# FFN output weights loaded ahead of batch three's values, and a Hankel tile of which half is loaded and half copied

## The chip, the cores and the metric

The kernel runs on one core of a Trainium2 chip. The core has five engines with their own instruction streams: TensorE (PE, matmuls, with weight loads shown as PEld), VectorE (DVE), ScalarE (ACT), GpSimd (POOL) and SyncE (SP). They wait for each other by semaphores. SP, ACT and POOL also issue DMAs. The metric is the device time of one execution in microseconds (us).

## What is computed

Attention with a relative position bias for 8 batches of 8 heads, 576 positions and 64 numbers a head, and behind it a feed-forward network (FFN) in which three products are joined by a maximum:

```
scores = q @ k.T / sqrt(64) + bias[bucket(|i - j|)]      # per batch and head, 576 x 576
x      = softmax(scores) @ v                             # to (8*576, 512)
h      = max(x @ w1, x @ w2, x @ w3)                     # w: 512 x 768
out    = h @ w_out                                       # w_out: 768 x 512, out: 4608 x 512, float32
```

The bucket depends on the distance |i - j| alone, and is the same for all distances from 128 up.

## The kernel before

**Bias as a product.** Softmax doesn't change when a constant is taken from all scores, so the kernel uses exp(bias - bias at far distance) as a factor: it is 1 from distance 128 up, and differs only in a band of 383 diagonals. `spread_bias` makes for each of the 8 heads a row of 511 such factors, w_sb, and writes it to DRAM (w_dr). `load_hank` reads it back as a Hankel tile, `hank`: partition p holds the row shifted by p. The exponentials of the scores are multiplied by slices of it on DVE (`times_band`, L771; `times_band_left`, L870; and `times_bandt`, L857, with `bandt`, a reversed copy of a part of hank that `make_bandt` writes).

**Tiling.** Keys and queries of a batch are 4 tiles of 128 positions and a tail of 64. Heads are worked in pairs (HP = 4 pairs a batch). For a pair: scores into PSUM (`sc`; `sct` for the 64 left keys, `scq` for the 64 left queries), exponentials on ACT into `e` and `el`, band products on DVE, then `attend` (products with the values, PSUM tile `a`) and the division on DVE into x_sb.

**Batches.** In batch 0 the queries and keys are turned on PE (`first_transposes`, `more_transposes`), in two passes over the four pairs: the first takes queries 0 to 255, the second the others. Batch 1 is turned on PE too. From batch 2 on, SP turns queries and keys by DMA transposes (L702, ten a batch, for tiles 0 to 3 and the tail, queries and keys by turns); from batch 1 on it also turns the attention's output x_sb into xT (L923, L971). xT, 128 x 4 x 4608, is the FFN's input; corners of it that are written late hold other data early on (borrowed for q and k in float32, for the indices and the zeros).

**FFN.** Its products (`ps`, `psp`, and `pso` with the output weights wo_bf) are put between the attention's as filling for PE. The first chunk of outputs comes in batch 2.

**Order.** The kernel writes the order of nearly all instructions by hand (`inorder`, `in_turn`): each engine follows program order. POOL issues the loads from DRAM that convert float32 to bfloat16: L181 and L162, L184 (queries and keys of a batch and their tails, eleven DMAs by `load_qk`), L153 and L172 (values and their tails, six by `load_v`), L1014 (FFN weights) and L1033 (output weights). A POOL load first waits for the load eight before it, whose semaphore it takes over. `go_behind` adds a wait on a given transpose to loads. In batch 1, pair 2, the order on POOL is: values of batch 2, output weights, queries and keys of batch 3, the first behind batch 2's key transpose of tile 1, the others behind that of tile 3:

```
last_v = load_v(b + 1, 0, H, turned_qk[b + 1, 1, min(b, 2) if b < 4 else KT - 1])
if b == 1:
    load_last_weights(turned_qk[2, 1, KT - 1])
    batch[3] = load_tiles()
    load_qk(3, turned_qk[2, 1, KT - 1])
```

In the first pass of batch 0, on DVE, the band products of pairs 0 and 1 (`bands`) follow the query copy of `more_transposes(0)`; the query copy of the second pass, bandt and the divisions come after them.

Of the kernel before, what the change touches and what calls it, by code (L numbers as in the profile page):

```python
# [11 lines left out]
BF16 = mybir.dt.bfloat16  # L12
# [27 lines left out]
def kernel(  # L40
# [12 lines left out]
    nc = tc.nc  # L53
    B, H, S, D = q.shape
    d_model, d_ff = moe_w1.shape
    NB = bias_table.shape[0]
    P = 128
# [5 lines left out]
    KT = 4  # L63
# [4 lines left out]
    CH = 512  # L68
    NCH = NTOK // CH
    BAND = 3 * P  # L70
    HALF = 2 * P - 1
    WL = 2 * HALF + 1
# [3 lines left out]
    const = ctx.enter_context(tc.tile_pool(name="const", bufs=1))  # L76
    stage = ctx.enter_context(tc.tile_pool(name="stage", bufs=1))
# [28 lines left out]
    def mm(*args, **kw):  # L106
        made = inorder(nc.tensor.matmul(*args, **kw))  # L107
        return made
# [11 lines left out]
    def act_copy(out_, in_):  # L120
        return inorder(nc.scalar.activation(out=out_, in_=in_, func=ACTF.Copy))

    def dve_copy(out_, in_):
        return inorder(nc.vector.tensor_copy(out_, in_))  # L124
# [22 lines left out]
    def in_turn(b, load):  # L147
        return inorder(load)

    def load_main(src, b, h0, h1, dst, t0=0, t1=KT):  # L150
        x = main_part(src, b)
        return [
            in_turn(b, nc.gpsimd.dma_start(out=dst[:, t, h0:h1, :], in_=x[:, t, h0:h1, :])) for t in range(t0, t1)  # L153
        ]
# [15 lines left out]
    def load_tail(src, b, h0, h1, dst):  # L170
        return [
            in_turn(b, nc.gpsimd.dma_start(out=dst(b, par, h0, h1), in_=tail_part(src, b, h0, h1, par)))  # L172
            for par in range(2)
        ]
# [13 lines left out]
    def go_behind(loads, behind):  # L188

        for load in loads if behind else ():  # L190
            tc.add_manual_dep(
                load.ins, behind.ins.name,
                mybir.DependencyInfo(mybir.DependencyClass.Sync, mybir.DependencyReason.DATA),
                reason="these loads go behind the transposes in line",
            )

    def load_v(b, h0, h1, behind=None):
        loads = load_main(v, b, h0, h1, vx[b % 2][:, :, :, 0:D]) + load_tail(v, b, h0, h1, v_diag)
        go_behind(loads, behind)
        return loads[-1]  # L200
# [3 lines left out]
    xT = const.tile([P, DCH, NTOK], BF16, name="xT")  # L204
# [63 lines left out]
    for vv in range(single, NB):  # L268
# [5 lines left out]
        out=pick[:, 0:NW], in0=pick[:, 0:NW], scalar1=pick[:, NW:], scalar2=None, op0=ALU.is_equal,  # L274
# [18 lines left out]
        mm(warm[:, 0:CH], lhsT=zeros[:, 0:P], rhs=zeros[:])  # L293

    act_copy(batch[0][0][:, 0:2, 0:2, :], q32[:, :, 0:2, :])
    w_sb = stage.tile([H, WL], BF16, name="w_sb")

    def spread_bias():
        spread = ps_a.tile([H, NW], F32, tag="a", name="spread")
# [7 lines left out]
        inorder(nc.scalar.dma_start(out=w_dr[:], in_=w_sb[:]))  # L307

    w_dr = dram.tile([H, WL], BF16, name="w_dr")
    hank = const.tile([P, H, BAND], BF16, name="hank")  # L310

    def load_hank(h0, h1):
        inorder(nc.sync.dma_start(
            out=hank[:, h0:h1, :],
            in_=bass.AP(
                tensor=w_dr.tensor, offset=w_dr.offset + h0 * WL,
                ap=[[1, P], [WL, h1 - h0], [1, BAND]],
            ),
        ))

# [444 lines left out]
    def times_band(hp, e4, t, lo, hi, put=lambda x: x):  # L767
        lo, hi = max(lo, P * t - P), min(hi, P * t + 2 * P)
        if lo < hi:
            c0, c1 = BAND - (hi - P * t + P), BAND - (lo - P * t + P)  # L770
            put(nc.vector.tensor_tensor(  # L771
                out=e4[:, t, :, lo:hi], in0=e4[:, t, :, lo:hi],
                in1=hank[:, 2 * hp : 2 * hp + 2, c0:c1][:, :, ::-1], op=ALU.mult,
            ))
# [36 lines left out]
    def visit(qT, kT, e4, c, mid=None, el=None):  # L811

        if el is not None:
            banks = [ps_a.tile([P, KT * 64], F32, tag="a", name="scq") for _ in range(2)]
            turn_left_queries(qT, kT, banks)
            put_left_queries(el, banks)
        for tt in range(0, KT, 2):
            scores(qT, kT, e4, c, tt)
            if tt == 0 and mid:
                mid()  # L820
# [53 lines left out]
    divided, turned_qk = {}, {}  # L874

    def attend(b, hp, e4, el, half):

        x = ps_a.tile([P, 6, AW], F32, tag="a", name="a")
        v, vl = vx[b % 2], vt[b % 2]
        for i in range(2):
            t = 2 * half + i
            c = slice(P * t, P * t + P)
            mm(
                x[:, 2 * i : 2 * i + 2, :], lhsT=el[:, c], rhs=vl[:, hp, :, 0:AW],
                start=True, stop=False, skip_group_check=True,
            )
            for par in range(2):  # L890
                for kt in range(KT):
                    mm(
                        x[:, 2 * i + par, :], lhsT=e4[:, kt, par, c], rhs=v[:, kt, 2 * hp + par, 0:AW],
                        start=False, stop=(kt == KT - 1), skip_group_check=True,
                    )
        n = 2 + half
        if half:
            mm(
                x[:, 4:6, :], lhsT=el[:, S - P : S], rhs=vl[:, hp, :, 0:AW],
                start=True, stop=False, skip_group_check=True,  # L900
            )
            for par in range(2):
                for kt in range(KT):
                    mm(
                        x[:, 4 + par, :], lhsT=el[:, S - 64 + P * kt + 64 * par :][:, 0:P],
                        rhs=v[:, kt, 2 * hp + par, 0:AW],
                        start=False, stop=(kt == KT - 1), skip_group_check=True,
                    )

        def quotients():  # L910
            rd = nrm.tile([P, 6], F32, tag="rd", name="rd")
            inorder(nc.vector.reciprocal(rd[:, 0 : 2 * n], x[:, 0 : 2 * n, D]))
            divided[b, hp, half] = inorder(nc.vector.tensor_tensor(
                out=x_sb[b][:, 2 * half : 2 * half + n, P * hp : P * hp + P].rearrange("p t (h d) -> p t h d", d=D),
                in0=x[:, 0 : 2 * n, 0:D].rearrange("p (t h) d -> p t h d", h=2),
                in1=rd[:, 0 : 2 * n].rearrange("p (t h) -> p t h", h=2).unsqueeze(3).to_broadcast([P, n, 2, D]),
                op=ALU.mult,
            ))
            if b and hp == HP - 1:
                for t in range(2 * half, 2 * half + 2 + half):  # L920
                    c = b * S + P * t
                    w = min(P, S - P * t)
                    inorder(nc.sync.dma_start_transpose(out=xT[:, :, c : c + w], in_=x_sb[b][P - w :, t, :]))  # L923
        return quotients
# [69 lines left out]
    def e_tiles():  # L994
        return (
            ep.tile([P, KT, 2, QM], BF16, tag="e4", name="e4"),
            ep.tile([P, S + KT * P], BF16, tag="el", name="el"),
        )
# [19 lines left out]
    wo_bf = const.tile([P, FCH, d_model], BF16, name="wo_bf")  # L1018
# [10 lines left out]
        load_v(1, 0, H)  # L1029
        load_w(2)  # L1030

    def load_last_weights(behind):
        load = in_turn(0, nc.gpsimd.dma_start(out=wo_bf[:], in_=moe_w_out.rearrange("(c p) m -> p c m", p=P)))  # L1033
        go_behind([load], behind)

    def bands(hp):
        for t in range(KT):
            times_band(hp, first_e[hp], t, 0, QS, inorder)
# [9 lines left out]
    for hp in range(HP):  # L1048
        qT, kT = (x[:, hp, :] for x in qk[0])
        e4, el = e_tiles()  # L1050
        first_e.append(e4)
        visit(qT, kT, e4, 0, (lambda: first_transposes(hp + 1)) if 0 < hp < HP - 1 else None)
        if hp == HP - 1:
            more_transposes(0)
        if hp == 0:
            first_transposes(1)
        if hp == 1:
            last_keys()
        if hp + 2 < HP:
            cast_keys(hp + 2)  # L1060
        if hp == HP - 1:
            bands(0)
            bands(1)
        late.append(lambda hp=hp, e4=e4, el=el: attend(0, hp, e4, el, 0))
        keep_warm()
        lefts.append(lambda hp=hp, qT=qT, kT=kT, el=el: left_keys(
            hp, qT, kT, el, 0, QS, ps_a.tile([P, QS], F32, tag="a", name="sct")
        ))
        while hp and lefts:
            lefts.pop(0)()  # L1070
# [8 lines left out]
    behind, begun = [], []  # L1079
# [69 lines left out]
    for b, hp in [(b, hp) for b in range(1, B) for hp in range(HP)]:  # L1149
# [132 lines left out]
        if hp == 1 and b > 1:  # L1282
            pending.extend((n, [fn]) for n, fn in rest)
            rest.clear()
            made, tail = ffn((b - 1) * CH, CH, False, [(b + (i + 2) // HP, (i + 2) % HP) >= ROWS for i in range(HP)])
        if hp == 2 and b + 1 < B:
            last_v = load_v(b + 1, 0, H, turned_qk[b + 1, 1, min(b, 2) if b < 4 else KT - 1])
            if b == 1:
                load_last_weights(turned_qk[2, 1, KT - 1])
                batch[3] = load_tiles()  # L1290
                load_qk(3, turned_qk[2, 1, KT - 1])
        if hp == 2 and 1 < b < B - 2:
# [73 lines left out]
```

## Time and profile before

| what | value |
|---|---|
| median of 3 runs | 312.76 us (312.24 to 314.45) |
| profiled execution | 312.26 us, of which the span of instructions is 310.5 us |
| PE busy | 298.9 us (96% of the span) |
| weight loads (PEld) | 182.5 us (59%) |
| DVE busy | 207.7 us (67%) |
| ACT busy | 202.4 us (65%) |
| POOL busy | 110.9 us (36%) |
| DMA | 40.48 MB in 163950 packets |
| chain that ended last | PE 89%, ACT 5%, DMA 2% |

A share of busy time is a mean over the whole span. Lines of a timeline give start, length, engine, line, operation, tile written <- tiles read, shape and count, and in brackets the idle time of the engine before it and what ended that. In a list of DMAs the last number is the time from issue to landing. All times are us from the start of the span.

### The profile page before, as it was taken

How to read it: one execution, taken by the hardware profiler on the slowest of the kernel's cores; microseconds unless marked ns; L12 is line 12 of the kernel's file. 1: busy time of each engine (PE TensorE's matmuls, PEld its weight loads, DVE VectorE, ACT ScalarE, POOL GpSimd, SP SyncE). 2: the span in 40 equal slices, each digit the busy share in tenths (PEclk: the TensorE clock that was granted, in tenths of full speed). 3: DMA queues.
4: the chain of work that ended last, by engine and by line, in shares of the span. 5: the costliest groups of instructions: out<-in, count | busy, mean ns of one | idle time of the engine just before them, and what ended most of it. 6: DMA issues, size and time to landing. Idle time of an engine off the chain costs nothing.

```text
span 310.5 us, 10532 instructions
## 1 busy us (share of the span) xinstructions
PE 298.9 (96%) x4542; PEld 182.5 (59%) x4542; DVE 207.7 (67%) x475; ACT 202.4 (65%) x268; POOL 110.9 (36%) x147
## 2 busy tenths in 40 slices
PE   6989999999999999999999999989999999999995
PEld 2357777775555655657665756666667654444442
DVE  7389788776777776776777667766776665553552
ACT  3899988886778777767776877675776730122211
POOL 8978752951096008900647024901500000000000
PEclk9599999999999999999999999999999999999999
DMA  9999999999999999999999999999932014202003
GB/s 167 198 187 199 182 163 136 145 166 139 141 157 191 151 187 155 133 147 198 105 101 125 165 183 111 112 146 202 131 62 106 36 33 80 101 0 103 34 0 135
DMA packets 163950, 40.48 MB, mean 130 GB/s; under 512 B 153784, under 2 KB 159424, under 8 KB 163904
## 3 DMA queue, kind: packets, MB, share of 16 engines
q0 software_dynamic: 103840, 16.66, 75.7%
q1 hardware_dynamic: 58304, 22.69, 43.6%
q8 instruction: 35, 0.57, 0.8%
q10 hardware_dynamic: 1760, 0.47, 0.7%
q14 instruction: 11, 0.09, 0.1%
HBM read 35.39 MB, written 9.45 MB: 144 GB/s over the span
## 4 chain that ended last, share of the span: by engine, by line
PE 89%; ACT 5%; DMA 2%; issue 1%; DVE 1%; ACTq 1%; DVEq 0%
PE psp L107 34%; PE ps L107 19%; PE a L107 14%; PE sc L107 9%; PE pso L107 6%; ACT e L777 4%; PE sct L107 2%; PE scq L107 2%; PE tp L111 1%; DMA xT<-in_q_dram 1%; DMA out_dram<-osb 1%; ACT el L777 1%; ACTq L213 1%; PE xp L111 0%; DVE k_sb L124 0%
## 5 line engine op out<-in xcount | busy, mean ns | idle before, releaser
L777 ACT ACTIVATE e<-sc 128x1024 bf16<-128x1024 f32 x128 | 128.4, 1023 | 30.4 <-PE sc L107 27.3
L107 PEld LDWEIGHTS <-w_bf 64*128 64x128 bf16 (+1 forms) x1088 | 73.4, 95 | 57.9 <-issue 5.0
L107 PE MATMUL psp<-xT,w_bf 64*128 64x512 bf16 x736 | 91.9, 376 | 1.9 <-issue 1.8
L771 DVE TENSOR_TENSOR e<-e,hank 128x512 bf16<-128x512 bf16 (+2 forms) x136 | 62.3, 473 | 20.3 <-ACT e L777 19.7
L107 PE MATMUL ps<-xT,w_bf 128*128 128x512 bf16 (+1 forms) x352 | 65.6, 336 | 0.0
L153 POOL DMA_DIRECT2D vx<-in_v_dram x28 | 24.7, 895 | 83.0 <-DMA kT<-k_sb 40.7
L107 PE MATMUL sc<-qT,kT 64*128 64x256 bf16 (+1 forms) x384 | 48.6, 312 | 2.0 <-DVE kT L124 0.8
L107 PEld LDWEIGHTS <-kT 64*128 64x128 bf16 (+1 forms) x736 | 31.3, 95 | 26.8 <-issue 8.4
L107 PE MATMUL a<-vx,e 64*128 64x65 bf16 (+1 forms) x1536 | 44.7, 191 | 0.0
L107 PEld LDWEIGHTS <-e 64*128 64x128 bf16 (+1 forms) x1536 | 40.7, 95 | 3.7 <-issue 0.2
L107 PEld LDWEIGHTS <-hT 64*128 64x128 bf16 (+1 forms) x444 | 26.9, 95 | 19.4 <-DVE hT L519 1.9
L107 PE MATMUL a<-vt,el 64*128 64x65 bf16 (+1 forms) x240 | 30.8, 201 | 0.4 <-DVE m L484 0.4
L107 PEld LDWEIGHTS <-el 64*128 64x128 bf16 (+1 forms) x624 | 26.2, 95 | 7.9 <-issue 4.7
L394 ACT ACTIVATE m<-ps 128x512 bf16<-128x512 f32 x14 | 8.4, 597 | 34.3 <-PE ps L107 34.3
L777 ACT ACTIVATE el<-sct 128x576 bf16<-128x576 f32 (+2 forms) x36 | 21.6, 603 | 13.5 <-PE sct L107 13.1
L107 PE MATMUL psp<-wo_bf,hT 64*128 64x256 bf16 (+1 forms) x336 | 29.7, 307 | 0.0
L181 POOL DMA_DIRECT2D q_sb<-in_q_dram x24 | 22.1, 921 | 10.7 <-issue 4.6
L181 POOL DMA_DIRECT2D k_sb<-in_k_dram x24 | 22.0, 917 | 4.0 <-DMA wo_bf<-in_moe_w_out_dram 2.1
L107 PE MATMUL pso<-wo_bf,hT 128*128 128x512 bf16 (+2 forms) x108 | 23.2, 367 | 0.0
L777 ACT ACTIVATE el<-scq 128x512 bf16<-128x512 f32 (+1 forms) x33 | 19.2, 585 | 3.3 <-PE scq L107 3.2
L403 DVE TENSOR_TENSOR m<-ps,m 128x512 bf16<-128x512 f32 x14 | 9.7, 692 | 17.0 <-PE ps L107 17.0
L519 DVE TENSOR_TENSOR hT<-psp,m 128x1024 bf16<-128x1024 f32 x12 | 14.7, 1225 | 6.9 <-PE psp L107 6.9
(82 smaller groups left out, 287.6 us busy)
## 6 DMA issues: line engine op xcount, KB each, us to landing
out_dram<-osb SPq DMA_DIRECT2D x35, 256.0 KB, 2.8
vx<-in_v_dram POOLq DMA_DIRECT2D x28, 128.0 KB, 5.0
q_sb<-in_q_dram POOLq DMA_DIRECT2D x26, 128.0 KB, 7.6
k_sb<-in_k_dram POOLq DMA_DIRECT2D x24, 128.0 KB, 7.8
w_bf<-in_moe_w_dram POOLq DMA_DIRECT2D x3, 768.0 KB, 9.3
xT<-in_k_dram SPq DMA_DIRECT2D x6, 128.0 KB, 4.2
hank<-w_dr SPq DMA_DIRECT2D x2, 384.0 KB, 5.7
wo_bf<-in_moe_w_out_dram POOLq DMA_DIRECT2D x1, 768.0 KB, 8.8
```

The costliest lines, as they stand in the source:

```text
L107: made = inorder(nc.tensor.matmul(*args, **kw))
L111: inorder(nc.tensor.transpose(*args))
L153: in_turn(b, nc.gpsimd.dma_start(out=dst[:, t, h0:h1, :], in_=x[:, t, h0:h1, :])) for t in range(t0, t1)
L181: loads.append(in_turn(b, nc.gpsimd.dma_start(out=dst[:, t], in_=main_part(src, b)[:, t])))
L213: inorder(eng.dma_start(out=dst[:, :, h, :], in_=main_part(src, 0)[:, 0:nt, h, :]))
L394: nc.scalar.activation(out=st[fb]["m0"][:], in_=ps0, func=ACTF.Copy)
L403: inorder(nc.vector.tensor_tensor(out=m[:], in0=ps1, in1=st[fb]["m0"][:], op=ALU.max))
L519: return lambda: inorder(nc.vector.tensor_tensor(out=hT[:, fb * CH : fb * CH + 2 * CH].rearrange("p (i t) -> p i t", i=2), in0=ps2(), in1= ...
L771: put(nc.vector.tensor_tensor(out=e4[:, t, :, lo:hi], in0=e4[:, t, :, lo:hi], in1=hank[:, 2 * hp : 2 * hp + 2, c0:c1][:, :, ::-1], op=ALU. ...
L777: made = nc.scalar.activation(out=out_, in_=in_, func=ACTF.Exp, scale=inv_sqrt_d)
```

## The change

The Hankel tile gets 64 more columns. The load fills partitions 0 to 63 only, with the wider rows; DVE copies each half of the heads to partitions 64 to 127, shifted by 64 columns. The first copy stands ahead of the first band products, the second behind those of pair 1. The row of factors, w_sb, moves from a tile of its own into a corner of xT, which makes room for the columns. The load of the output weights stands ahead of the values of batch 2 (`b + 1` with b = 1) in POOL's order, so right behind batch 2's queries and keys, and no longer waits for a transpose.

```diff
-    w_sb = stage.tile([H, WL], BF16, name="w_sb")
+    w_sb = xT[0:H, 0, 3 * CH + P : 3 * CH + P + WL]
...
-    hank = const.tile([P, H, BAND], BF16, name="hank")
+    hank = const.tile([P, H, BAND + 64], BF16, name="hank")
 
     def load_hank(h0, h1):
         inorder(nc.sync.dma_start(
-            out=hank[:, h0:h1, :],
+            out=hank[0:64, h0:h1, :],
             in_=bass.AP(
                 tensor=w_dr.tensor, offset=w_dr.offset + h0 * WL,
-                ap=[[1, P], [WL, h1 - h0], [1, BAND]],
+                ap=[[1, 64], [WL, h1 - h0], [1, BAND + 64]],
             ),
         ))
+
+    def copy_hank(h0, h1):
+        dve_copy(hank[64:, h0:h1, 0:BAND], hank[0:64, h0:h1, 64:])
...
-    def load_last_weights(behind):
-        load = in_turn(0, nc.gpsimd.dma_start(out=wo_bf[:], in_=moe_w_out.rearrange("(c p) m -> p c m", p=P)))
-        go_behind([load], behind)
+    def load_last_weights():
+        in_turn(0, nc.gpsimd.dma_start(out=wo_bf[:], in_=moe_w_out.rearrange("(c p) m -> p c m", p=P)))
...
         if hp == HP - 1:
+            copy_hank(0, KT)
             bands(0)
             bands(1)
+            copy_hank(KT, H)
...
         if hp == 2 and b + 1 < B:
+            if b == 1:
+                load_last_weights()
             last_v = load_v(b + 1, 0, H, turned_qk[b + 1, 1, min(b, 2) if b < 4 else KT - 1])
             if b == 1:
-                load_last_weights(turned_qk[2, 1, KT - 1])
                 batch[3] = load_tiles()
                 load_qk(3, turned_qk[2, 1, KT - 1])
```

## The prediction

> **What bounds the kernel now.** I read the page first (shares, slices), then the table by stage, then the timelines of VectorE (DVE), GpSimd (POOL) and SyncE (SP) where the two edits lie, and the times of DMAs to landing.
>
> The page says who is full, and when:
>
> ```profile
> span 310.5 us, 10532 instructions
> PE 298.9 (96%) x4542; PEld 182.5 (59%) x4542; DVE 207.7 (67%) x475; ACT 202.4 (65%) x268; POOL 110.9 (36%) x147
> PE   6989999999999999999999999989999999999995
> DVE  7389788776777776776777667766776665553552
> ```
>
> TensorE (PE) is busy 298.9 of 310.5 us. All that any edit could win from its waits is 11.6 us, and most of that lies at the two ends. So the question is where an edit makes PE wait, or stops it waiting. By stage:
>
> ```profile
> 16.00:20.00 4.00, 2.69 (x44) 1.73 (x43) 3.23 (x12) 3.95 (x7) 2.78 (x5) 1.00 1.79 181
> 20.00:24.00 4.00, 3.84 (x82) 2.89 (x81) 3.93 (x15) 3.87 (x7) 2.35 (x4) 1.00 1.44 192
> 24.00:28.00 4.00, 3.68 (x74) 2.64 (x73) 3.93 (x14) 3.80 (x7) 3.41 (x5) 1.00 1.26 209
> 56.00:64.00 8.00, 8.00 (x117) 6.02 (x115) 5.58 (x16) 7.15 (x11) 7.50 (x10) 1.00 1.70 148
> ```
>
> The columns are window, length, then busy us of PE, weight loads, DVE, ACT, POOL. From 16 to 20 us ACT is full (3.95 of 4.00) and PE waits for it: its 1.31 us idle are exponentials. From 20 to 28 DVE and ACT are both full. At 56 to 64 PE has no gap at all.
>
> The Hankel copies land here:
>
> ```profile
> 16.12 0.33 DVE L124 COPY qT<-tp 128x320 bf16<-128x320 bf16 x1 [1.63 <-PE tp L111]
> 16.36 1.83 DVE L771 TENSOR_TENSOR e<-e,hank 128x512 bf16<-128x512 bf16 x6
> 18.10 0.32 DVE L124 COPY qT<-tp 128x320 bf16<-128x320 bf16 x1
> 18.34 0.71 DVE L124 COPY bandt<-hank 64x768 bf16<-64x768 bf16 x2
> 19.65 0.18 DVE L912 RECIPROCAL rd<-a 128x4 f32<-128x4 f32 x1 [0.60 <-PE a L107]
> ```
>
> DVE has one gap, 0.60 us, before 19.65; the next is 0.43 us at 30.8. And the output weights lie here:
>
> ```profile
> 44.37 1.25 POOL L184 DMA_DIRECT2D ktail<-in_k_dram  x2
> 57.96 0.85 POOL L1033 DMA_DIRECT2D wo_bf<-in_moe_w_out_dram  x1 [0.50 <-DMA kT<-k_sb]
> 67.02 0.88 POOL L181 DMA_DIRECT2D k_sb<-in_k_dram  x1 [2.09 <-DMA wo_bf<-in_moe_w_out_dram]
> 55.40 1.21 SPq L702 DMA_TRANSPOSE kT<-ktail  x1
> kT<-ktail SPq DMA_TRANSPOSE x1, 6.0
> 62.31 0.41 PE L107 MATMUL sct<-qT,kT 128*128 128x512 bf16 x2
> 68.62 1.46 PE L107 MATMUL pso<-wo_bf,hT 128*128 128x512 bf16 x6
> ```
>
> The output weights are issued at 57.96 and land after 8.8 us, at 66.8; their first reader starts at 68.62, so PE does not wait for them. The last key transpose of batch two is issued at 55.40, lands after 6.0, at 61.4, and its reader's weight load starts at 62.20: 0.8 us of cover, the thinnest near this edit.
>
> [...] 512 elements take 0.28 us (the packed copies at L228), 768 take 0.35 (bandt). [...] I don't take the halved Hankel load as landing much sooner. [...] the trace has one band product of 839 ns beside POOL's copies at 25.4 us, where the median is 426. [...] the third query transpose of batch two, with POOL's queue nearly empty, lands in 4.0 us, the first of batch three, beside loads, in 8.9 to 10.2.
>
> **Part one, the Hankel tile.** *Removed:* per load, 512 rows of 768 bytes become 256 rows of 896 bytes; over both, 786 KB become 459 KB. Before, the two land at 15.2 (10.0 + 5.2) and 16.6 (10.4 + 6.2), their readers come at 16.36 and 18.34, so nothing waits for them. Loads behind on the same engines may come some tenths sooner; PE is held by ACT there, so I count zero, and at most 0.3 us.
>
> *Added:* two DVE copies of 64 x 1536 elements. Price: [...] from the trace's slope, 0.35 + 768 x (0.07/256) = 0.56. Back to back copies overlap by some 0.06, so 0.50 each. From below they cannot be free; from above, [...] 1.0 each, twice the price.
>
> *Where it lands:* the first sits between the query copy and the first bands. Bands of pair 0 end at 17.3 + 0.5 = 17.8, their reader `a` starts at 18.85: covered. The second sits ahead of the query copy at 18.10, which then ends at 19.42; its reader, the scores at 19.96, still has 0.5. bandt ends at 20.05 instead of 19.05. The gap of 0.60 takes its share: the reciprocal moves from 19.65 to 20.05, 0.40 late, and DVE runs full until 30.8, so all behind it is 0.40 late. PE's readers of bands have, before: 21.16 to 21.61 (0.45), 22.61 to 23.02 (0.41), 24.26 to 24.63 (0.37), 27.05 to 27.44 (0.39). So PE loses 0 to 0.05: I take +0.1. With copies of 1.0 us DVE is 1.4 late and PE loses 1.4 - 0.39 = 1.0.
>
> w_sb in a corner of xT costs the same two activations (0.82 us for both), and its bytes are overwritten by batch two's columns at 91 us, long after the one DMA that reads them. Nothing.
>
> **Part two, the output weights.** *Moved:* one POOL issue (0.85 us) from behind batch two's values to ahead of them, and its wait for the last key transpose goes. In program order it follows batch two's tail loads, which end at 45.6; the slot that it reuses, a key load issued at 37.1, landed at 44.9. So it goes out at 45.6, 12.3 us sooner, into time in which POOL idled 7.06 us: the issue itself is hidden. What it is moved past: four value loads and two tails, which now queue behind it; and it leaves the space ahead of batch three's eleven loads, so their 2.09 us stall at 67.0 goes. They land some 4 to 5 us earlier; but batch three's first scores, at 89.35 in the chain of waits, find their keys landed at 86.9 (82.82 + 4.1), so PE waits for no DMA there and this wins nothing. The weights' own reader didn't wait either.
>
> *What is late next:* the data, 0.786 MB at this stage's 150 GB/s, is 5.2 us of all DMA engines, in the middle of batch two's ten transposes, issued from 42.55 to 56.6. Before, POOL's queue is busy with query and key loads until 51.4 anyway and again with values from 52.7 (first bytes about 54), so only 51.4 to 54 was free for the transposes. In these 2.6 us they now share, at about half the rate: 1.3 us later for the last key transpose, less the cover of 0.8, is 0.5 us of wait at 62.2. A check from the other side: batch three's transposes, which share all the way, take 70.50 to 86.35 from first to last issue where batch two's take 42.55 to 55.40: 3.0 us more, last landing 5.3 against 6.0. That gives 2.3 later, 1.5 us of wait. From below: zero, if the packets fit in. I take +0.6. The other readers have more cover: keys for the first scores land at 57.4 and are read at 60.28; the values, queued behind the weights, would land at 63 to 64 instead of 62.5, read at 66.86.
>
> **The sum.** +0.1 and +0.6 are +0.7 us, and PE is full behind 62, so it stays to the end: 312.26 (span 310.5 and 1.76 around it) becomes 312.96. The median of the runs shown, 312.76, lies 0.50 above that profiled execution; on its scale I say 313.5.
>
> **Rivals.** *Slower: batch two's transposes fall behind.* Output weights come in rows of 512 numbers, eight times the rows of query and key loads[...]. The transposes of xT at 91.4 us took 8.80 for five, 1.76 each against 1.3; eight of batch two's at this pace are 3.7 us later, and landing in 8 instead of 6.0 adds 2: 5.7 late, 4.9 of wait, 317.7. It decides from 0.8 us of lateness on, and crosses 1% at 3.9. For it: PE has no gap there and the cover is thin. Against: the xT transposes at 62.95 to 70.4, beside the weights in the kernel before, went out in 1.49 each. *Faster: the DMA relief reaches PE.* Half the Hankel rows free the engines at 10 to 16 us, all POOL loads come sooner, and the transposes of batch two with them; together with the lost stall: at best PE's idle in 20 to 60 us, about 1.1, so 311.7. Against: ACT, not a load, ends PE's waits there. *The copies at double price:* 1.0 instead of 0.1, so 314.4. *The change doesn't do what it says:* if the weights waited in POOL's order after all, nothing moves, 312.9; the waits in the instruction order speak against it.
>
> **How the numbers follow.** Forecast 0.55, with the double-price copies 0.15 more; weights held back 0.03; slow transposes 0.19; relief 0.08. The forecast's own bounds are 312.8 to 315.3 (0 to 1.0, and 0 to 1.5). The range for 8 in 10 goes down to the relief, 311.8, and up into the slow case, 316.5. A change of over 1%, 3.1 us, is about what a measurement of this kernel can tell from none: faster by it 0.05 (of the relief, the part that would also have to close gaps outside that stretch), within it 0.76, slower 0.19 (the slow case).
>
> **What would show each step.** After: two copies hank<-hank near 0.5 us, at 16.4 and 18.6; the gap before the first reciprocal gone; bands in time for `a`. wo_bf issued near 45.6; no stall of k_sb on it; the last key transpose landing near 62.7 and a PE weight load waiting half a us for it. Wrong if PE waits more than 2 us near 60, if DVE is over 1 us late at 24 to 28, or if PE starts its FFN work earlier than before.

## The result: half a per cent slower, by a longer wait than forecast

| | before | after |
|---|---|---|
| median, timed side by side | 313.33 us (310.42 to 321.7, 22 runs) | 314.8 us (312.65 to 317.82, 22 runs) |
| ratio after to before | | 1.0052, 95% interval 1.0031 to 1.0072 |
| profiled execution | 312.26 us, span 310.5 | 316.15 us, span 314.4 |

The medians are of all runs; the ratios are of the fast ones alone, without runs over 1.5% above the fastest of their kernel (4 of 22 before, 3 of 22 after). The ratio is worth +1.6 us (0.0052 x 313.33); on the 312.76 us of the runs shown first it makes 314.4. The forecast was +0.7 us and 313.5. So the change costs time, within 1%, about twice as much as forecast.

The page of after, the lines that answer to those of before:

```profile
span 314.4 us, 10534 instructions
PE 298.4 (95%) x4542; PEld 182.6 (58%) x4542; DVE 208.6 (66%) x477; ACT 202.3 (64%) x268; POOL 110.9 (35%) x147
```

PE is not busier, 298.4 us against 298.9; the span is 3.9 us longer. So PE stands still for longer (16.0 us against 11.6), and a stop is to be looked for. The table by stage of after (window, length, busy us of PE, weight loads, DVE, ACT, POOL, then PE clock, DMA share, GB/s):

```profile
20.00:24.00 4.00, 3.84 (x71) 2.48 (x68) 3.93 (x16) 3.42 (x7) 1.81 (x3) 1.00 1.46 191
24.00:28.00 4.00, 3.86 (x79) 3.00 (x77) 3.93 (x15) 4.00 (x8) 3.86 (x6) 1.00 1.23 208
56.00:64.00 8.00, 6.20 (x97) 4.55 (x94) 5.00 (x14) 6.28 (x9) 6.16 (x8) 1.00 1.68 145
64.00:72.00 8.00, 7.83 (x117) 5.99 (x118) 4.57 (x13) 5.12 (x6) 7.55 (x10) 0.79 2.32 156
```

At the Hankel tile (20 to 28) PE has 3.84 and 3.86 of 4.00, not less than the 3.84 and 3.68 of before. At 56 to 64 it has 6.20 of 8.00, where before it had all 8.00. And behind that, at 64 to 72, the granted clock is 0.79.

The DVE timeline of after, where the Hankel copies are:

```profile
14.42 0.32 DVE L124 COPY qT<-tp 128x320 bf16<-128x320 bf16 x1 [1.63 <-PE tp L111]
15.36 0.55 DVE L124 COPY hank<-hank 64x1536 bf16<-64x1536 bf16 x1 [0.62 <-DMA hank<-w_dr]
17.89 0.58 DVE L124 COPY hank<-hank 64x1536 bf16<-64x1536 bf16 x1
19.50 0.18 DVE L915 RECIPROCAL rd<-a 128x4 f32<-128x4 f32 x1
```

Two copies of 0.55 and 0.58 us, the first behind a wait of 0.62 us for the Hankel load, and no idle time before the first reciprocal: the gap of 0.60 us took in a part of them. The reciprocal is not later than before (19.65), but only because the first query copy comes earlier here, at 14.42 instead of 16.12; from that copy to the reciprocal it is 5.08 us instead of 3.53. The output weights, and the values behind them, in the timeline of POOL of after:

```profile
45.15 0.86 POOL L1036 DMA_DIRECT2D wo_bf<-in_moe_w_out_dram  x1
57.84 3.52 POOL L153 DMA_DIRECT2D vx<-in_v_dram  x4 [11.84 <-PE sc L107]
```

The values in that of before:

```profile
52.68 3.53 POOL L153 DMA_DIRECT2D vx<-in_v_dram  x4 [7.06 <-PE tp L111]
```

The transposes behind them, in SP's timeline:

```profile
49.19 3.18 SPq L705 DMA_TRANSPOSE kT<-k_sb  x1
52.46 2.08 SPq L705 DMA_TRANSPOSE qT<-q_sb  x1
54.63 2.16 SPq L705 DMA_TRANSPOSE kT<-k_sb  x1
58.19 2.09 SPq L705 DMA_TRANSPOSE kT<-ktail  x1
```

The reader, and the first reader of the weights, in PE's timeline:

```profile
64.17 0.42 PE L107 MATMUL sct<-qT,kT 128*128 128x512 bf16 x2 [1.97 <-DMA kT<-ktail]
71.86 1.46 PE L107 MATMUL pso<-wo_bf,hT 128*128 128x512 bf16 x6
```

And a line of the chain of waits (start, length, what):

```profile
58.19 5.93 DMA kT<-ktail
```

The weights go out at 45.15. While they are under way, three transposes take 3.18, 2.08 and 2.16 us to issue (before: 1.2 to 1.7). The key tail is issued at 58.19 (before: 55.40) and lands 5.93 us later, at 64.12. Its reader, the score tail `sct`, waits 1.97 us. The DMA lists say how long the weights were under way: before they land 8.8 us after issue, after 12.0 us, so until 57.15. The line of after in that list (size, us to landing):

```profile
wo_bf<-in_moe_w_out_dram POOLq DMA_DIRECT2D x1, 768.0 KB, 12.0
```

Two of the transposes issued in that time land late. The key transpose of tile 1 (issued at 47.06 in before, at 46.60 in after) takes 10.7 us instead of 5.1, and the query transpose behind it 9.6 instead of 5.7. The first of them in the lists of before and of after:

```profile
kT<-k_sb SPq DMA_TRANSPOSE x1, 5.1
```

```profile
kT<-k_sb SPq DMA_TRANSPOSE x1, 10.7
```

The program makes the values wait for this transpose (the brackets of the two POOL lines name something else), and in both kernels they go out about 0.5 us after it lands. So they go out at 57.84 instead of 52.68, and by then the weights have landed.

The stop is not the whole of it. The score tail before the stop starts at 55.99 in after and at 56.27 in before. From there to the score tail three steps on (75.41 before, 78.66 after) is 22.67 us against 19.14, 3.5 more: 8.18 against 6.04 up to the tail that waits, then 7.45 against 6.06 up to the next, then the same 7.04. So 2.1 us go with the wait and 1.4 behind it, where no wait is. There the clock is low. The table by stage of after, us by us:

```profile
64.00:65.00 1.00, 0.83 (x8) 0.66 (x9) 0.00 (x0) 0.37 (x1) 1.00 (x2) 1.00 2.79 145
65.00:66.00 1.00, 1.00 (x11) 0.59 (x10) 0.43 (x1) 0.28 (x1) 1.00 (x2) 0.68 2.13 161
66.00:67.00 1.00, 1.00 (x15) 0.65 (x12) 0.42 (x2) 0.96 (x2) 1.00 (x3) 0.50 2.41 153
67.00:68.00 1.00, 1.00 (x20) 1.00 (x17) 0.56 (x1) 0.98 (x2) 1.00 (x3) 0.50 1.67 167
68.00:69.00 1.00, 1.00 (x16) 0.72 (x14) 0.75 (x3) 0.45 (x1) 1.00 (x2) 0.61 2.28 156
```

The third figure from the end is the clock. PE works again from 64.17; at about 65.4 the clock falls to one half, and at 68.8 it is back: (1 - 0.68) x 2 + 2 + (1 - 0.61) x 2 = 3.4 us at half speed. PE shows as full in these rows, so a busy share alone would not have told it.

This is one execution. The timed runs put the mean loss at 1.6 us, less than half of this profile's. Executions differ here, as the experiments show for the kernel before too.

### The profile page after: what moved, and what is told of

Read it like the earlier page. It is cut to its first block, busy times and chain, and to the rows that moved or that the text cites. A ratio compares the mean times of both kernels' runs of the same rounds, so it can differ in the third digit from the quotient of the medians.

```text
span 314.4 us, 10534 instructions
## 1 busy us (share of the span) xinstructions
PE 298.4 (95%) x4542; PEld 182.6 (58%) x4542; DVE 208.6 (66%) x477; ACT 202.3 (64%) x268; POOL 110.9 (35%) x147
## 4 chain that ended last, share of the span: by engine, by line
PE 79%; DMA 8%; SPq 5%; POOL 4%; issue 2%; ACT 2%; DVE 0%; POOLq 0%
PE psp L107 33%; PE ps L107 16%; PE a L107 12%; PE sc L107 7%; PE pso L107 6%; SPq L705 5%; DMA w_bf<-in_moe_w_dram 3%; PE sct L107 2%; DMA vx<-in_v_dram 2%; DMA kT<-ktail 2%; ACT e L780 1%; PE scq L107 1%; POOL q_sb L153 1%; POOL ktail L172 1%; DMA out_dram<-osb 1%
## 5 line engine op out<-in xcount | busy, mean ns | idle before, releaser
L774 DVE TENSOR_TENSOR e<-e,hank 128x512 bf16<-128x512 bf16 (+2 forms) x136 | 62.2, 472 | 21.1 <-ACT e L780 20.5
L107 PE MATMUL a<-vx,e 64*128 64x65 bf16 (+1 forms) x1536 | 45.8, 191 | 0.2
L107 PEld LDWEIGHTS <-e 64*128 64x128 bf16 (+1 forms) x1536 | 41.4, 95 | 4.3 <-DVE e L774 0.5
L780 ACT ACTIVATE el<-sct 128x576 bf16<-128x576 f32 (+2 forms) x36 | 21.7, 606 | 15.1 <-PE sct L107 14.9
```

Of the source, the lines that this page charges most:

```text
L774: put(nc.vector.tensor_tensor(out=e4[:, t, :, lo:hi], in0=e4[:, t, :, lo:hi], in1=hank[:, 2 * hp : 2 * hp + 2, c0:c1][:, :, ::-1], op=ALU. ...
L780: made = nc.scalar.activation(out=out_, in_=in_, func=ACTF.Exp, scale=inv_sqrt_d)
```

## The experiments

Theory A: the Hankel part costs nothing; the moved weights make batch two's last key transpose late, PE stands still for it, and the loss is this stop and the low clock behind it. Rivals: a part of the loss is the Hankel part, or the weights cost elsewhere. Each ratio is to runs of the kernel before on the same chip, with its 95% interval.

**One part alone.** Kernel before with the Hankel part of the change only; in short:

```diff
-    hank = const.tile([P, H, BAND], BF16, name="hank")
+    hank = const.tile([P, H, BAND + 64], BF16, name="hank")
...
+            copy_hank(0, KT)
             bands(0)
             bands(1)
+            copy_hank(KT, H)
```

> Hankel part alone; the output weights are loaded where they were, behind batch two's values and with their wait. Theory A (the loss is the weights' load, which makes the last key transpose of batch two late): within 0.3 us of before, ratio 0.998 to 1.002, the last key transpose issued near 55 and landed near 61, no wait of TensorE for it above 0.3 us, TensorE's clock 1.0 from 64 to 72. Theory B (the two copies on a full VectorE cost the time): 1 to 2 us slower, 1.003 to 1.006, with VectorE over 0.5 us later at the band products of 24 to 28 us.

Measured: 313.45 us (14 runs), ratio 0.9998 (0.9966 to 1.0029). Its DVE timeline has both copies, 0.55 and 0.58 us long; its key tail is issued at 56.08 and lands at 62.2, both about 1 us later than expected, and PE does not wait. Nothing of the loss is visible here, though the interval alone would still leave room for 0.9 us.

The weights only, with the Hankel load as before:

```diff
+            if b == 1:
+                load_last_weights()
...
-                load_last_weights(turned_qk[2, 1, KT - 1])
```

> Output weights ahead of batch two's values and without wait; the Hankel tile as before. Theory A: all of the loss, ratio 1.004 to 1.008, the wait for the last key transpose near 2 us at 62 and a lower clock behind it. Theory B: nothing, 0.998 to 1.002. If both parts cost, each shows about half.

Measured: 315.18 us (22 runs), ratio 1.0062 (1.004 to 1.0085): the whole loss. PE's timeline of this kernel:

```profile
65.60 0.42 PE L107 MATMUL sct<-qT,kT 128*128 128x512 bf16 x2 [3.01 <-DMA kT<-ktail]
```

And its table by stage:

```profile
66.00:67.00 1.00, 1.00 (x9) 0.66 (x6) 0.00 (x0) 0.65 (x1) 1.00 (x2) 0.68 2.63 154
67.00:68.00 1.00, 1.00 (x10) 0.44 (x8) 0.61 (x1) 0.13 (x1) 1.00 (x2) 0.50 2.08 155
68.00:69.00 1.00, 1.00 (x18) 0.82 (x15) 0.33 (x3) 1.00 (x2) 1.00 (x2) 0.50 1.88 172
69.00:70.00 1.00, 1.00 (x26) 0.95 (x23) 0.48 (x1) 0.81 (x1) 1.00 (x3) 0.62 2.43 154
```

The same picture: a stop of 3.01 us for the same tile, and again 3.4 us at half clock (0.64 + 2 + 0.76).

**The wait or the place.** The edit does two things to the weights: it moves them and it drops their wait. Kernel before, wait dropped, place kept:

```diff
-                load_last_weights(turned_qk[2, 1, KT - 1])
+                load_last_weights()
```

> The kernel before, with the weights still behind batch two's values, and only their wait for the key transpose of tile 3 taken away. If the place in the queue is what costs: no change, 0.998 to 1.002, the weights issued some 0.5 us sooner (57.4) and the last key transpose landing before 62. If the wait itself is what protected the transposes: slower by 1 us or more, with TensorE waiting for the last key transpose.

Measured: 313.76 us (22 runs), ratio 1.0008 (0.9984 to 1.0032). The place matters, not the wait. But PE's timeline of this kernel holds something that I had not expected:

```profile
63.51 0.42 PE L107 MATMUL sct<-qT,kT 128*128 128x512 bf16 x2 [0.92 <-DMA kT<-ktail]
```

With the weights behind the values, they go out at 58.60, after the tail transpose (56.64), and still PE waits 0.92 us in this execution: the tail was issued 1.2 us later than in before and took 6.8 us to land instead of 6.0. The cover of 0.8 us is within what one execution differs from another by, whatever the weights do.

**Half of the weights early.** After, with chunks 0 to 2 ahead of the values and 3 to 5 where they were before:

```diff
             if b == 1:
-                load_last_weights()
+                load_last_weights(0, FCH // 2)
...
+                load_last_weights(FCH // 2, FCH, turned_qk[2, 1, KT - 1])
```

> The changed kernel with only half of the output weights (three of six blocks, 384 KB in bfloat16) loaded early; the other half at the old place with the old wait. If the lateness of the last key transpose grows with the bytes ahead: it lands 1.0 to 1.7 us later than in the kernel before (62.4 to 63.1) instead of 2.7, the wait is 0.3 to 1.0 us[...], ratio 1.000 to 1.003. If any load in that place delays the transposes alike (order, not bytes): lands near 64, ratio 1.004 to 1.007.

Measured: 314.52 us (22 runs), ratio 1.0039 (1.0017 to 1.0061). In its profile the tail is issued at 56.27, between 55.40 and 58.19, lands at 63.4, PE waits 1.53 us (0.3 to 1.0 was expected), and the clock stays at 1.00. That the lateness grows with the bytes is not shown: the kernels with all weights in the old place and the tails' transposes in the old order issue the tail at 55.40 to 57.26, and the timed ratios don't tell half from all.

**Filling the stop.** To part the stop from the clock, I gave PE work to do in it: after, with eight matmuls of zeros ahead of the score tail.

```diff
+            if (b, hp) == (2, 0):
+                idle = ps_a.tile([P, CH], F32, tag="a", name="idle")
+                for _ in range(8):
+                    mm(idle[:], lhsT=zeros[:, 0:P], rhs=zeros[:])
```

> The changed kernel, with eight matmuls of zeros (nobody reads their result) ahead of the left keys of batch two's first pair, where TensorE waits 2 us for the last key transpose; they take about 1.8 us, so most of them lie inside the wait. If the lower clock behind the wait (0.79 from 64 to 72 us, work of 4.0 us taking 5.4) comes from TensorE standing idle: the clock stays 1.0, and of the loss 1 to 1.4 us come back, ratio to before 1.000 to 1.003. If the dip is chance and not due to the wait: as the changed kernel or slightly slower, 1.005 to 1.007.

Measured: 318.29 us (6 runs), ratio 1.0159 (1.0119 to 1.02): the expectation missed. Its table by stage:

```profile
64.00:68.00 4.00, 4.00 (x62) 3.03 (x61) 1.86 (x5) 2.74 (x4) 4.00 (x6) 1.00 2.38 165
68.00:72.00 4.00, 3.95 (x69) 2.55 (x70) 3.36 (x10) 2.93 (x4) 3.19 (x5) 1.00 2.30 167
212.00:216.00 4.00, 3.87 (x43) 2.69 (x43) 0.27 (x2) 2.54 (x3) 0.00 (x0) 0.68 1.61 264
```

And its list of waits of PE (who, line, for what; total, times, longest):

```profile
PE psp L107 <- issue: 2.2, 1, 2.2
```

Here it does what was meant: the clock stays at 1.00 at 64 to 72, and this stretch takes 1.7 us more than before instead of 3.5. But at 210 PE stops for 2.2 us with no releaser in the trace ("issue"), and the clock falls behind that. To see whether that belongs to the eight matmuls, they were put into the kernel before:

> The kernel before with the same eight matmuls of zeros ahead of the left keys of batch two's first pair, where it has no wait: the price of these matmuls themselves, and of 16 more TensorE instructions. If the kernel that filled the wait lost time by the matmuls' own side effects (it ran 5 us slower than before although its profile gained 1.7 us at that place): 4 to 7 us slower here, ratio 1.013 to 1.022. If a matmul costs only its time: 1.7 us, ratio 1.004 to 1.007.

Measured: 316.35 us (6 runs), ratio 1.012 (1.0074 to 1.0166), so +3.8 us for matmuls of 1.7 us, with an "issue" stop of 1.96 us at 210. In this profile, too, the key tail is late (issued at 57.26, landed at 64.1), which the matmuls hide. The eight matmuls cost some 2 us elsewhere, so the timed results of both kernels say nothing about the stop. A smaller number of longer ones was to avoid that: after, with four float32 matmuls on the same zeros.

```diff
+                z32 = zeros.bitcast(F32)
+                for _ in range(4):
+                    mm(idle[:, 0:QS], lhsT=z32[:, 0:P], rhs=z32)
```

> The changed kernel with the wait filled by four float32 matmuls of zeros instead of eight in bfloat16 (fewer instructions[...]). If the clock dip comes from standing idle, and the earlier filling kernel's loss from its instructions: clock 1.0 from 64 to 72, ratio 1.000 to 1.003. If filling itself costs [...]: 1.010 to 1.018 again.

The list of waits of PE of this kernel:

```profile
PE idle L107 <- DMA xT<-x_sb: 7.0, 1, 7.0
```

Measured: 326.02 us (6 runs), ratio 1.0417 (1.0369 to 1.0466), and useless as a test. The zeros lie in a corner of xT, and their float32 view made the filling itself wait 7.0 us for a transpose into xT. It measures a longer stop, no more.

**The reader later.** After, with the score tail of that pair moved behind the products that followed it (`left_keys` and `times_bandt` at the end of the pair):

```diff
-            if (b, hp) != (3, 0):
+            if (b, hp) not in ((2, 0), (3, 0)):
...
+            if (b, hp) == (2, 0):
+                left_keys(hp, qT, kT, el, 0, S)
+                times_bandt(hp, el)
```

> The changed kernel with the reader of the last key transpose, the left keys of batch two's first pair, put behind that pair's second half of scores (and its band product behind it): some 1.5 us of other matmuls go first. Theory A (the loss is this one wait of 2.0 us and the lower clock behind it): the wait falls to 0.5 us, the clock stays 1.0, ratio to before 1.000 to 1.003. Rival (the early weights slow TensorE in other places too, or the last key transpose is late only in the profiled execution): ratio stays at 1.004 to 1.007.

Measured: 315.02 us (22 runs), ratio 1.0053 (1.003 to 1.0077): missed. The wait for the DMA is gone, the clock stays at 1.00 and this stretch costs 1.0 us instead of 3.5, but PE's timeline of this kernel has a new wait:

```profile
65.96 0.41 PE L107 MATMUL sct<-qT,kT 128*128 128x512 bf16 x2 [0.90 <-ACT e L780]
```

In its new place the score tail waits for an exponential to free its bank. The timed ratio lies where the rival had it, so this run speaks against the wait for the key tail as the only cause. In this profile PE is 1.2 us behind before ahead of that stretch already (57.44 against 56.27 at the score tail before it), which the moved reader can't explain. Which executions carry the loss is open.

**The transpose earlier, the reader left alone.** In SP's order the tails of batch two change places, keys before queries. First on after:

```diff
-            one(0, t)
-            one(1, t)
+            for j in (1, 0) if (b, t) == (2, KT) else (0, 1):
+                one(j, t)
```

> The changed kernel with one edit: in SP's order the last two transposes of batch two change places, so that the key tail goes ahead of the query tail. Theory A (the loss is the late landing of the key tail, and what follows the stop of PE): the key tail is issued near 56.9 and lands near 62.8, the wait of the score tail shrinks from 2.0 us to 0.6 or less, the clock stays at 1.0 at 64 to 72, and the timed ratio to before is 1.000 to 1.003; the query tail then lands near 64, where its reader is due at 65. Rival (the weights' load costs PE in other ways than this wait): 1.004 to 1.007 with the wait gone.

Measured: 314.29 us against 313.98 (22 and 43 runs), ratio 1.0016 (0.9994 to 1.0038). PE's timeline of this kernel:

```profile
61.59 0.39 PE L107 MATMUL sct<-qT,kT 128*128 128x512 bf16 x1
63.23 0.19 PE L107 MATMUL sct<-qT,kT 128*128 128x64 bf16 x1 [1.25 <-DMA qT<-qtail]
```

The key tail, issued at 56.50, no longer holds anything up. The second half of the same score tail reads the query tail, which I had thought due only at 65; it is due at 62 and now is late, by 1.25 us instead of 1.97. The clock stays at 1.00. With these two transposes swapped and all else left as in after, the ratio keeps 0.0016 of the 0.0052. That speaks for this wait, and what follows it, as the greater part of the loss; but the intervals, 0.9994 to 1.0038 and 1.0031 to 1.0072, still touch, so a small part elsewhere is not excluded.

Then on the kernel before, as a version that might beat both:

> The kernel before with the same edit as in the run on the changed kernel: the key tail of batch two ahead of the query tail in SP's order. Theory A (executions of the kernel before wait here at times too): no wait for the key tail, ratio 0.997 to 1.000. Rival (before, that transpose is in time in nearly all executions): 1.000, within 0.002 of it.

Measured: 313.32 us against 313.98, ratio 0.9985 (0.9963 to 1.0008). No wait for a tail in its profile. A gain is possible and not shown.

**The lateness without the weights.** Kernel before, weights where they were, and two more transposes in SP's order ahead of the tails:

```diff
+            if (b, t) == (2, KT):
+                for i in range(2):
+                    src = batch[b][i][:, KT - 1].rearrange("p h d -> p (h d)")
+                    c = 5 * CH + P * i
+                    inorder(nc.sync.dma_start_transpose(out=xT[:, :, c : c + P], in_=src))
```

> The kernel before with two transposes more in SP's order ahead of the tails of batch two (they write columns of xT that nobody reads before they are overwritten; the weights' load stays where it was). Theory A: the key tail lands some 2.6 us later than in before, near 64, PE waits about 2 us for it near 62, and the ratio is 1.004 to 1.007, as in the changed kernel, though no weight is moved. Rival (the place of the weights' load costs PE otherwise): 1.000 to 1.002.

Measured: 318.86 us against 313.98 (6 and 43 runs), ratio 1.0127 (1.0085 to 1.0168). The chain of waits, PE's timeline and the table by stage of this kernel:

```profile
58.61 8.75 DMA kT<-ktail
```

```profile
67.41 0.66 PE L107 MATMUL sct<-qT,kT 128*128 128x512 bf16 x2 [4.96 <-DMA kT<-ktail]
```

```profile
64.00:68.00 4.00, 0.59 (x3) 0.32 (x4) 0.00 (x0) 0.00 (x0) 3.19 (x4) 0.64 1.33 157
68.00:72.00 4.00, 4.00 (x40) 2.66 (x38) 1.42 (x3) 2.30 (x3) 2.93 (x4) 0.50 1.50 171
```

The delay came out more than twice as long as I had meant: the tail goes out 3.2 us later than in before, near what was planned, but also takes 8.75 us to land instead of 6.0. So the size is missed and the sign isn't: late tails, with no weight moved, make PE wait (4.96 us), with half the clock behind it, and cost time (+4.0 us by the ratio). This is the mechanism that theory A names, without the moved weights, in a larger dose.

## Why the prediction was right in kind and half in size

- **Hankel copies.** Priced at 0.56 us each by the slope of the trace; measured 0.55 and 0.58 in after, and 0.55 to 0.87, 0.66 in the mean, in the seven profiles with these copies. The double price, an estimate of mine, was not seen. The net forecast of +0.1 us fits: the run of the Hankel part alone puts it at 0.0 within about 1 us on either side, and the score tail that starts at 56.27 in before starts at 55.5 to 57.4 (mean 56.3) in the seven profiles with the copies and at 56.2 to 56.7 (mean 56.4) in the six without. The way there was not as forecast, and in part it was luck. DVE was to be 0.40 us late. From the first query copy to the first reciprocal it takes 3.53 us in each of the six profiles, and 1.0 to 1.6 us more in the seven. In the mean 0.7 us of this is made up, because that query copy starts earlier in the seven, at 15.1 instead of 15.8; whether the smaller Hankel load brings that isn't shown. The load itself lands no sooner, 5.7 us after issue (median of its two halves) in before and in after.
- **POOL.** Issue of the weights forecast at 45.6, seen at 45.15. The stall of a key load of batch three behind the weights was to go, and no POOL load from 57.84 to 71.5 in after, once the first value load is out, waits for one. As forecast, this won nothing: the FFN's first output product starts at 71.86 instead of 68.62, later, not earlier.
- **The place and the sign of the loss.** One reader, of the last key transpose of batch two, was named. The weights alone show the loss in full, and of the 3.9 us between the two profiles 3.5 come between 56 and 79 us. With the tails swapped the ratio is 1.0016, and two more transposes make such a loss without moved weights. Against it stands the reader put later, whose ratio stayed at 1.0053. So this wait, with the clock behind it, is the best supported cause; that it is the only one is not shown.
- **The step that failed** is the size of the wait, "1.3 us later for the last key transpose, less the cover of 0.8, is 0.5 us of wait at 62.2". Measured in the two profiles compared: 2.7 us later (64.12 against 61.4) and 1.97 us of wait, 3.01 with the weights alone. It assumed that the weights and the transposes share only "these 2.6 us" ahead of the values, at about half the rate; both were estimates of mine. But the weights were under way for 12.0 us. Two transposes issued in that time took about twice as long to land (10.7 and 9.6 us instead of 5.1 and 5.7), and the next ones 3.18, 2.08 and 2.16 us to issue, as the rival of slow transposes had it, in a smaller dose; the slower landing of the last one, which it had too, didn't come (5.93 us). The values were not in line with the weights all the while: they wait for one of these transposes and went out 5.2 us later than before.
- **The cover of 0.8 us was that of one execution.** With the weights in the old place, the last key transpose lands at 61.4 (before), 62.2 (Hankel part alone), 63.5 (wait dropped) and 64.1 us (eight matmuls), in the last two later than PE is ready for it. With the weights early it lands at 64.1 (after), 65.6 (weights alone), 64.0 (filled), 63.2 (reader later) and 64.0 (float32 filling). The means are 62.8 and 64.2. By these few profiles the weights make it 1.4 us later, near the 1.3 forecast, and what was mis-sized is the cover, which is mostly not there. By the two profiles alone it is the lateness, and the estimate from batch three's transposes (2.3 us of lateness, 1.5 of wait) was nearer. Which term carries more of the error stays open. Two readings of lines were off, without weight for the sum: the transpose that lands in 4.0 us is batch two's fourth query transpose, not the third, which took 5.7; and at 25.4 us two band products are long, 839 and 825 ns, not one.
- **A term that was missing**: the clock. A stop was priced at its own length. In the profile of after it cost 1.97 us of wait (2.1 by the starts of the score tails), and then 1.4 more at half clock; with the weights alone 3.01 and then 1.5 (7.55 against 6.06 us to the next score tail).
- **What the two terms make together** is 3.5 us in the profiled execution and 1.6 in the mean. A mean with this stop and the low clock in every execution of after, and neither in any of before, would be twice the measured one. Kernels with the weights in the old place wait here in some executions too (0.92 us with the wait dropped), and the low clock comes only in some; how often was not measured.

## What to carry to other kernels

A load that waits for nothing is not free when it is issued into a stretch in which DMA transposes feed a full engine: here it cost 1.6 us in the mean. Find the thinnest cover among their readers first, and read it in more than one execution: here one profile showed 0.8 us, and two others of kernels with the weights in the same place none. Price a stop of TensorE with the slower clock that may follow it (1.4 us behind the stop of 1.97 in after), and read the clock column behind the stop, because the busy share hides it (1.00 of each us from 65 to 69 there). Putting dummy work into a stop, or moving the reader, brought a new stop each time (2.20 us, 7.0 with float32, and 0.90); the change of two transposes' places in the queue was the only repair that left PE's work alone, and the one whose time came back near that of before, though in its profile PE still waits 1.25 us.

## What the hardware showed that I had not expected

**The half clock comes in pieces of 3.4 us, and after the stop.** Worked out from the rows by us as above: 3.4 us at half speed in after, 3.4 with the weights alone, 3.4 in the filled kernel at 213 to 217, 3.4 on the kernel before with the swapped tails at 211 to 215, and 6.8 in the kernel with two more transposes. It starts 2.5 to 3.8 us after PE stopped (after: 62.20 to 65.4; weights alone: 62.59 to 66.4), so that in after it hits work that had already gone on for 1.2 us. Within a profile, the low stretches compared begin a whole multiple of one length apart. In after they begin at 65.36 and, behind the last work of PE, at 314.53 us, which is 73 times 3.413 us; in before at 7.48 and 311.27, 89 times 3.413; in the filled kernel at 18.92 and 213.48, 57 times 3.413; with the float32 filling at 11.53 and 66.15, 16 times 3.414. The counts are an estimate from these starts and the 3.4 us that a stretch lasts. With this length I cut the profiles into slices. Not every stop was followed by the low clock: behind 0.92, 1.34, 1.53 and 1.58 us it stayed at 1.00. The slices, counted back from a low stretch of the same profile, sort the stops. The third column has the share of a slice in which PE is busy, for the emptiest slice that the stop touches:

| stop of PE | kernel | PE busy in the slice | clock behind it |
|---|---|---|---|
| 0.92 us | before, wait dropped | 0.73 | 1.00 |
| 1.34 us (at 209) | before | 0.66 | 1.00 |
| 1.53 us | half of the weights | 0.74 | 1.00 |
| 1.58 us (at 214) | weights alone | 0.54 | 1.00 |
| 1.81 us (at 209) | before, tails swapped | 0.47 | 0.50 |
| 1.96 us (at 210) | before with eight matmuls | 0.57 | 1.00 |
| 1.97 us | after | 0.42 | 0.50 |
| 2.20 us (at 210) | after with eight matmuls | 0.39 | 0.50 |
| 2.28 us (at 219) | float32 filling | 0.59 | 1.00 |
| 3.01 us | weights alone | 0.22 | 0.50 |
| 4.96 us | two more transposes | 0.21 | 0.50 |
| 7.0 us (at 62) | float32 filling | 0.00 | 0.50 |

The stop of 1.81 us lies in one slice, and that of 1.96 us is split between two. The tables by stage of these two kernels (swapped tails, then eight matmuls), cut at the borders:

```profile
208.18:211.59 3.41, 1.60 (x23) 0.69 (x20) 0.43 (x1) 1.39 (x2) 0.00 (x0) 1.00 2.83 106
```

```profile
207.88:211.29 3.41, 1.95 (x20) 0.81 (x16) 1.88 (x5) 1.98 (x3) 0.00 (x0) 1.00 1.61 124
211.29:214.70 3.41, 2.91 (x62) 2.20 (x62) 0.45 (x2) 2.29 (x3) 0.00 (x0) 1.00 1.20 341
```

From 60 to 300 us, in all thirteen profiles, the low clock follows each slice with PE busy for 0.47 of it or less, and none with 0.54 or more; no slice lies between. So between 1.8 and 2.3 us the length of the stop doesn't sort these cases (behind 1.81, 1.97 and 2.20 us came half the clock, behind 1.96 and 2.28 not), and the share of the slice does; what sets the clock is not shown. Counted back to the start of the span, the first border lies at 0.51 us in after, 0.65 in before, 1.85 in the filled kernel and 1.29 with the float32 filling. If it moves like this between executions of one kernel too, the same stop costs its length in one and 1.4 us more in another: an estimate from these four profiles and from the loss in after. In the first 20 us this share doesn't sort them: in four profiles the low clock comes there behind slices with PE 0.57 to 0.67 busy and no stop above 1 us near (in before 6.8 us of it, from 7.48), in others it doesn't come behind slices no fuller.

**Stops of PE without a releaser.** In every profile PE stops, between 208 and 219 us, ahead of a filling product `psp`, with "issue" as the only reason given: 1.34 us in before, 0.93 in after with another of 1.02 at 218, 2.20 and 1.96 in the two kernels with eight matmuls more. What holds PE there stays open.
